# A mixture-of-experts kernel: guards moved behind another tile, eight index tiles, another order of an output's products

## The chip, the cores and the metric

The kernel runs on one core of a Trainium2 chip. The metric is the device time of one execution in microseconds (us). The kernel before took 802.78 us (median of three runs: 800.07, 802.78 and 802.8 us).

A core has five engines that run at the same time, each through its own list of instructions in order: PE (TensorE, matrix products), DVE (VectorE), ACT (ScalarE), POOL (GpSimd) and SP (SyncE, which here only issues DMAs). An instruction that must wait for another engine or for a DMA holds up everything behind it on its own engine.

## The reference, cut to what matters

The first half is a recurrence over 768 steps for 4 x 8 heads of 40 numbers; its output, laid out as 3072 rows of 320, goes into a mixture of eight experts:

```
state = state * w[t] - outer(state @ a[t], b[t]) + outer(v[t], k[t])
y[t]  = r[t] @ state                       # 4 x 8 heads, 40 x 40 state
x     = y as [3072, 320]
logits= x @ w_gate + log1p(exp(x @ w_noise)) * noise
top2  = the two best of 8 experts; weights = softmax over the two
for e in range(8): for k in range(2):
    rows = top2[:, k] == e
    out[rows] += weight[rows] * (relu(x[rows] @ w1[e]) @ w2[e])   # 320 -> 1024 -> 320
```

## The kernel before, in words

The recurrence fills the first 400 us of the span. The experts follow, from about 400 to 788 us, and a short check (`verdict`) ends the program. The change lies in the experts.

**Numbers in two halves.** Every float32 operand of the experts is split into two float16 tiles, a high part and a low part (the rest): the weights of the first product into `w1h` and `w1l`, of the second into `w2h` and `w2l`, the rows into `xh`, `xl` and, for the last 64 of the 320 columns, `x3` and `x3l`, the hidden layer into `hh` and `hl`. A product is then a sum of high by high, high by low and low by high.

**Tiles of an expert.** An expert has room for 832 rows in two parts (`PARTS`): 384 rows (part 0) and 448 rows (part 1). For each part `hidden` computes eight blocks of 128 hidden columns. A block (`block`, L348 to L357) is eight matmuls into one PSUM tile `ph` (three buffers): two of `wh` by `xh`, one by `x3`, two of `wl` by `xh`, two of `wh` by `xl`, one by `x3l`. ACT makes `hh` of it (L356), DVE makes `hl` (L357), and with that the buffer is free for the block that is three later. `trans` and `turn` transpose the rows on PE (L335, PSUM `pt`, two buffers), ACT makes `xh` and `x3` (L338, L341), DVE `xl` and `x3l` (L339, L342). `split1` and `split2` split weights (ACT L284 and L295, DVE L285, L286 and L296).

**Output tiles.** `output` goes over an expert's rows in tiles of 128, with one of 64 at the end. `otile` (L362 to L375) sums 24 matmuls of 128 by 320 in PSUM `po` (three buffers): eight of `hh` by `wh`, eight of `hl` by `wh`, eight of `hh` by `wl`. The 64-row tile does it in halves, 48 matmuls of 160 columns. ACT scales the sum by the row's weight into `y` (L372), and POOL adds `y` into the output in DRAM by a scatter with row indices (`add`, L378). For the 64-row tile, whose two halves lie on different partitions, DVE first computes an index tile `ix` (L374) out of the expert's row list: a tile called `ix2` of the pool `my`, which has two buffers. A third one can so be written only when the scatter of the first has landed.

**Row lists.** A list tile `le` holds an expert's row numbers and weights. It has three buffers and is filled by four small DMAs on SP (`lists`, L307: two for the 128-row tiles, two for the 64-row tile). POOL's `gather` (L313) fetches the rows by it.

**Guards.** Beside the sums run checks that the float16 halves are good enough: `sized` (L239, a maximum of a tile into `mx`), `finite` and `check1` (L242, a sum over the low parts into `yc`), and `flag` (L390 to L412: small operations on DVE named `ok`, `fz` and `g`, and small matmuls). Nothing waits for their results before the verdict.

**Order.** The names in the trace are those of memory: for even experts W1's halves and the rows read `rk` and `rw__68`, for odd ones `la`, `X__71` and `dr`; `ra` is W2 of expert 0. Of the experts the programmer writes only dependences and a few places; the order on each engine is chosen by the framework's scheduler when the program is built, which simulates the program by costs of its own. Places are given by `after(i, e)`, a dependence of one instruction upon another, and by `with issue_after(i):`, which lets the scheduler put what is inside only behind `i`. In `rest` (L438 to L464) the guards of the first expert stand in three such blocks, held behind `hx`:

```
s.trans(x[0],0,X,1); hx=s.hx3.ins; H1=s.hidden(W1,X,1,p)
with after(hx):
    for i in range(2): s.sized(s.x[i][0][:,0])
with after(hx): s.check1(W1)
      with after(hx): s.flag(s.pt,"pt",2,gam)
```

There `s.hx3` is the last DVE instruction that wrote `x3l`, that of expert 0, part 1.

Of the kernel before, what the change touches and what calls it, by code (L numbers as in the profile page):

```python
# [11 lines left out]
I32 = mybir.dt.int32  # L12
AF = mybir.ActivationFunctionType
ALU = mybir.AluOpType
# [38 lines left out]
class Moe:  # L53
# [275 lines left out]
    def after(s,i,e): s.tc.add_manual_dep(i.ins,e.ins.name,mybir.DependencyInfo(mybir.DependencyClass.Sync,mybir.DependencyReason.DATA),reason="place")  # L329
# [32 lines left out]
    def otile(s,W,H,wi,part,t,p,po,y):  # L362
        nc=s.nc; wh,wl=W; hh,hl=H; _,w_,idx=wi[:3]
        t0=s.parts[part][0]%CAP
        r=slice(t-t0,t-t0+p); ii=t//128
        c=128//p; d=DM//c
        k=0
        for h,w in ((hh,wh),(hl,wh),(hh,wl)):
            for f in range(8):
                for j in range(c): nc.tensor.matmul(po[p*j:p*j+p,:d],h[:,f,r],w[:,f,d*j:d*j+d],start=k==0,stop=k==23)  # L370
                k+=1
        s.hy=nc.scalar.activation(y[:,:d],po[:,:d],AF.Copy,scale=w_[:,ii:ii+1])  # L372
        if c==1: return s.out_d,idx[:,ii],y
        ix=s.yp.tile([128,1],I32,name="ix2"); nc.vector.scalar_tensor_tensor(ix,idx[:,ii],2.0,s.half2,op0=ALU.mult,op1=ALU.add)  # L374
        return s.out_d.rearrange("n (j d)->(n j) d",j=2),ix,y[:,:d]  # L375
    def add(s,o,e):
        s.finite(o[2])
# [60 lines left out]
    def rest(s,W1,W1n,W2,W2n,X,Xn,x,xn,ll,gam):  # L438
        after=s.tc.issue_after; p=s.places[5::2]; s.output(W2n,s.H,xn,1,0,p)
        for i in range(5): s.after(s.piece1(2,i),p[i])  # L440
        s.trans(x[0],0,X,1); hx=s.hx3.ins; H1=s.hidden(W1,X,1,p); s.after(s.piece1(2,5),p[5])
        for k,g in enumerate(s.gather(1,xn,1)): s.after(g,p[3+k])
        with after(s.hmm.ins): s.trans(xn[0],1,Xn,1)
        s.output(W2,H1,x,0,1)
# [3 lines that stand above are left out]
        W1,X,W2,x=W1n,Xn,W2n,xn  # L448
        for e in range(1,E_):
            if e+1<E_:  # L450
              r1=s.load1(e+1) if e>1 else s.w1s
              xn=s.loadx(e+1,places=p[7:10] if e==1 else ()); s.loadx(e+1,xn,1,p[10:] if e==1 else ()); r2=s.load2(e+1) if e>1 else s.r2
            if e>1: H0=s.hidden(W1,X,0)
            H1=s.hidden(W1,X,1); W1o=W1
            if e+1<E_: W1=s.split1(r1,e+1); X=s.trans(xn[0],e+1); s.trans(xn[0],e+1,X,1)
            if e>1: s.output(W2,H0,x,e,0)
            if e==1:
              with after(hx): s.flag(s.pt,"pt",2,gam)
            s.output(W2,H1,x,e,1); s.check1(W1o)
            if e+1<E_: W2=s.split2(r2,e+1); x=xn  # L460
# [651 lines left out]
```

## Time and profile before

| | |
|---|---|
| profiled execution | 800.72 us |
| its span, first to last instruction | 798.9 us |
| mean granted TensorE clock (share of full speed) | 0.974 |
| PE busy | 728.6 us, 91% of the span, 12622 matmuls |
| DVE busy | 495.0 us, 62% |
| ACT busy | 401.9 us, 50% |
| POOL busy | 348.7 us, 44% |
| blocks' matmuls L355 | 97.0 us + 86.4 us in two groups |
| PE po L370 on the chain that ended last | 21% of the span |

The span is 1.82 us shorter than the time of the execution. Busy shares are averages over two very different halves: in the first the engines hand small results to each other, in the second PE is the engine that others serve. The rows below say, for single instructions or for runs of equal ones (x24 is 24 of them), when the run began, how long it took, and in square brackets how long the engine stood idle before it and what ended that.

### The profile page before, as it was taken

What the parts mean: (1) busy time and instruction counts of PE and PEld (TensorE: products, weight loads), DVE (VectorE), ACT (ScalarE), POOL (GpSimd) and SP (SyncE); (2) the same over time, 40 slices, a digit from 0 to 9 for tenths busy, and PEclk for the clock granted to TensorE, in tenths of its full rate; (3) what the DMA queues carried; (4) which work ended last, traced back from release to release, by engine and by line L of the source; (5) the groups of instructions that cost most, each with busy time, mean ns of one, the idle gap of its engine ahead of it and who ended that gap; (6) DMA issues with size and microseconds to landing.
All of it is one profiled execution on the core that took longest, in us unless ns stands there. A gap on an engine that the chain in (4) does not pass through costs nothing.

```text
span 798.9 us, 29160 instructions
## 1 busy us (share of the span) xinstructions
PE 728.6 (91%) x12622; PEld 532.5 (67%) x12622; DVE 495.0 (62%) x1059; ACT 401.9 (50%) x876; POOL 348.7 (44%) x470
## 2 busy tenths in 40 slices
PE   7579999999999999898889898999999999999993
PEld 4367778888877777676655465657566675766662
DVE  7926667677989857935564675856565654652221
ACT  6765667676757444455442254454335434442220
POOL 9922143345367444325257544416345251503223
PEclk9699999999999999999999999999999999999997
DMA  6452344545544632352316664626445162402113
GB/s 203 149 133 70 100 143 149 157 143 162 156 132 127 196 104 58 105 154 66 93 58 128 140 145 125 152 77 130 125 112 142 41 143 71 50 5 34 22 21 39
DMA packets 67700, 87.07 MB, mean 109 GB/s; under 512 B 15640, under 2 KB 52460, under 8 KB 67564
## 3 DMA queue, kind: packets, MB, share of 16 engines
q1 hardware_dynamic: 55404, 67.98, 29.0%
q0 software_dynamic: 12160, 17.15, 12.8%
q8 instruction: 101, 1.65, 0.9%
q14 instruction: 35, 0.29, 0.1%
HBM read 63.41 MB, written 21.69 MB: 107 GB/s over the span
## 4 chain that ended last, share of the span: by engine, by line
PE 74%; ACT 9%; DVE 8%; issue 4%; DMA 2%; another core or an unknown queue 1%; POOL 1%; SPq 0%; ACTq 0%; DVEq 0%; POOLq 0%
PE po L370 21%; PE ph L355 20%; PE py L793 4%; PE pp L777 4%; PE rl L808 2%; PE pt L335 2%; PE sm L596 2%; PE tb L708 2%; ACT la L526 2%; PE ta L698 2%; PE kt L722 2%; ACT dr L526 2%; PE pw L739 2%; ACT tt L526 1%; PE pw L730 1%
## 5 line engine op out<-in xcount | busy, mean ns | idle before, releaser
L378 POOL DMA_INDIRECT out_dram<-y,le x45 | 74.5, 1656 | 176.4 <-ACT y L372 173.0
L355 PE MATMUL ph<-rw__68,rk 128*128 128x384 f16 (+1 forms) x512 | 97.0, 339 | 2.9 <-DVE hl L357 1.8
L355 PE MATMUL ph<-dr,la 128*128 128x448 f16 (+1 forms) x384 | 86.4, 341 | 1.7 <-DVE rk L357 1.2
L370 PEld LDWEIGHTS <-rk 128*128 128x128 f16 x576 | 56.1, 99 | 31.1 <-ACT rk L356 2.8
L355 PEld LDWEIGHTS <-rk 128*128 128x128 f16 x512 | 49.5, 98 | 39.4 <-issue 3.3
L182 POOL DMA_INDIRECT ls<-ent,po x48 | 49.6, 1034 | 54.3 <-ACT pm L526 33.3
L357 DVE SCALAR_TENSOR_TENSOR hl<-ph,hh 128x448 f16<-128x448 f32 x64 | 39.4, 621 | 49.9 <-ACT hh L356 49.2
L372 ACT ACTIVATE y<-po,le 128x320 f32<-128x320 f32 (+1 forms) x53 | 26.6, 504 | 86.7 <-PE po L370 77.3
L356 ACT ACTIVATE hh<-ph 128x448 f16<-128x448 f32 x64 | 34.2, 542 | 68.6 <-PE ph L355 64.8
L356 ACT ACTIVATE rk<-ph 128x384 f16<-128x384 f32 x64 | 30.9, 488 | 60.6 <-PE ph L355 48.5
L618 POOL TENSOR_TENSOR rk<-rk,B 104x512 f32<-104x512 f32 x34 | 40.4, 1191 | 42.8 <-DVE lg L812 41.3
L370 PEld LDWEIGHTS <-hh 128*128 128x128 f16 (+1 forms) x640 | 46.6, 103 | 18.7 <-issue 1.8
L646 DVE TENSOR_TENSOR Tt<-X__71 128x30 f32<-128x30 f32 (+9 forms) x150 | 54.3, 362 | 3.7
L355 PEld LDWEIGHTS <-la 128*128 128x128 f16 x384 | 37.5, 98 | 28.3 <-issue 2.6
L242 DVE TENSOR_REDUCE yc<-y 128x1 f32<-128x320 f32 (+1 forms) x53 | 23.8, 456 | 49.3 <-ACT y L372 49.2
L647 DVE TENSOR_TENSOR X__71<-X__71,Tt 128x30 f32<-128x30 f32 (+9 forms) x150 | 50.7, 338 | 5.5
L357 DVE SCALAR_TENSOR_TENSOR rk<-ph,rk 128x384 f16<-128x384 f32 x64 | 34.4, 552 | 31.2 <-ACT rk L356 25.1
L793 PE MATMUL py<-pm,kt 128*64 128x104 f32 (+1 forms) x768 | 43.5, 261 | 6.1 <-issue 4.6
L370 PE MATMUL po<-ra,rk 128*128 128x320 f16 x288 | 45.7, 305 | 2.9 <-ACT rk L356 2.4
L793 PEld LDWEIGHTS py<-pm,kt 128*64 128x64 f32 x768 | 36.7, 142 | 10.5 <-issue 7.4
L779 DVE TENSOR_TENSOR pm<-pp,mk 128x1024 f32<-128x1024 f32 x24 | 29.4, 1223 | 19.0 <-PE pp L777 18.2
L313 POOL DMA_INDIRECT rk<-xd,le x28 | 28.1, 1005 | 24.5 <-ACT hh L356 6.7
(330 smaller groups left out, 1726.1 us busy)
## 6 DMA issues: line engine op xcount, KB each, us to landing
rk<-in_gkb_dram SPq DMA_DIRECT2D x48, 160.0 KB
w2r<-in_w_dram SPq DMA_DIRECT2D x6, 1280.0 KB
w1s<-in_w_dram SPq DMA_DIRECT2D x28, 256.0 KB
xd<-xr SPq DMA_DIRECT2D x40, 160.0 KB
w1s<-in_w_dram SPq DMA_DIRECT2D x5, 1024.0 KB
out_dram<-z SPq DMA_DIRECT2D x15, 320.0 KB
rw__68<-in_gw_dram SPq DMA_DIRECT2D x24, 160.0 KB
ra<-in_ga_dram SPq DMA_DIRECT2D x48, 80.0 KB
```

Source lines behind the costliest of these rows:

```text
L182: st=nc.gpsimd.indirect_dma_start(out=s.ls,out_offset=OFFS(ap=po[:,j,k:k+1],axis=0),in_=s.ent[:,j,k],in_offset=None)
L355: for i,(a,b) in enumerate(mm): s.hmm=nc.tensor.matmul(ph[:,:n],a,b,start=i==0,stop=i==7)
L356: s.hrelu=nc.scalar.activation(hh[:,f],ph[:,:n],AF.Relu)
L357: s.hhl=nc.vector.scalar_tensor_tensor(hl[:,f],ph[:,:n],0.0,hh[:,f],op0=ALU.max,op1=ALU.subtract)
L370: for j in range(c): nc.tensor.matmul(po[p*j:p*j+p,:d],h[:,f,r],w[:,f,d*j:d*j+d],start=k==0,stop=k==23)
L378: st=s.nc.gpsimd.indirect_dma_start(out=o[0],out_offset=OFFS(ap=o[1],axis=0),in_=o[2],in_offset=None,compute_op=ALU.add)
L526: s.ea=s.nc.scalar.activation(*a,**k)
L618: s.after((eng or s.nc.gpsimd).tensor_tensor(z,z,b1,op=ALU.mult),e)
L646: eng.tensor_tensor(t,X[:,j:j+1,j+1:].to_broadcast([128,j,m]),X[:,0:j,j:j+1].to_broadcast([128,j,m]),op=ALU.mult)
L647: s.hs=eng.tensor_tensor(X[:,0:j,j+1:],X[:,0:j,j+1:],t,op=ALU.add)
L777: nc.tensor.matmul(pp[o:o+64,y,64*j:64*j+64],lh,r[Y,j],start=True,stop=True)
L793: nc.tensor.matmul(pp[64*y:64*y+64,b,128*hh:128*hh+n],kt[:,j,y],m[:,y,j,0:n],start=first and hh==0,stop=True,skip_group_check=True)
```

## The change

Three edits. In `otile` the products of an output tile come in the order high by high, `hh` by `wl`, `hl` by `wh`, where `hl` came second. The index tile `ix2` gets eight buffers of its own. And `hx` is taken behind `s.hidden(W1,X,1,p)`, as `s.hhl`, the DVE instruction that wrote the last `hl` of expert 0, part 1 (L357).

```
-        for h,w in ((hh,wh),(hl,wh),(hh,wl)):
+        for h,w in ((hh,wh),(hh,wl),(hl,wh)):
             for f in range(8):
                 for j in range(c): nc.tensor.matmul(...)
...
-        ix=s.yp.tile([128,1],I32,name="ix2"); nc.vector.scalar_tensor_tensor(ix,idx[:,ii],2.0,s.half2,...)
+        ix=s.yp.tile([128,1],I32,name="ix2",bufs=8); nc.vector.scalar_tensor_tensor(ix,idx[:,ii],2.0,s.half2,...)
...
-        s.trans(x[0],0,X,1); hx=s.hx3.ins; H1=s.hidden(W1,X,1,p); s.after(s.piece1(2,5),p[5])
+        s.trans(x[0],0,X,1); H1=s.hidden(W1,X,1,p); hx=s.hhl.ins; s.after(s.piece1(2,5),p[5])
```

The number of instructions stays the same; the scheduler puts them in another order on PE, DVE and ACT, and in the same order on POOL and SP.

On DVE, around the last blocks of expert 0, part 1 (`hl_8525`; the first two rows are transposed rows of that part), before:

```order
L339 SCALAR_TENSOR_TENSOR rw__68<-pt,rw__68 128x448 x2
L342 SCALAR_TENSOR_TENSOR rw__68<-pt,rw__68 64x448 x2
L239 TENSOR_REDUCE mx<-rk 128x1
L239 TENSOR_REDUCE mx<-rw__68 128x1
L242 TENSOR_REDUCE yc<-rk 128x1
L242 TENSOR_REDUCE yc<-rk 64x1
L390 MEMSET ok 128x5
L392 TENSOR_TENSOR fz<-acc 128x128
L402 TENSOR_TENSOR g_8959<-gam 128x216
L357 SCALAR_TENSOR_TENSOR hl_8525<-ph,hh_8524 128x448 x3
L393 TENSOR_SCALAR fz<-fz 128x128
```

The same place on DVE now (`dr` are rows of expert 1, part 1; `rk<-w1s` is the split of expert 2's W1):

```order
L357 SCALAR_TENSOR_TENSOR hl_8525<-ph,hh_8524 128x448 x8
L239 TENSOR_REDUCE mx<-rk 128x1
L239 TENSOR_REDUCE mx<-rw__68 128x1
L242 TENSOR_REDUCE yc<-rk 128x1
L242 TENSOR_REDUCE yc<-rk 64x1
L390 MEMSET ok 128x5
L392 TENSOR_TENSOR fz<-acc 128x128
L339 SCALAR_TENSOR_TENSOR dr<-pt,dr 128x448
L402 TENSOR_TENSOR g_8959<-gam 128x216
L339 SCALAR_TENSOR_TENSOR dr<-pt,dr 128x448
L285 SCALAR_TENSOR_TENSOR rk<-w1s,rk 128x1024 x2
```

All eight `hl` now come ahead of the guards, and the guards among the work for experts 1 and 2.

On DVE, where the weights of an odd expert have been split and the rows of the next are being transposed (`dr`), before (the index tile `ix_11058` is that of expert 5):

```order
L296 SCALAR_TENSOR_TENSOR w2l<-w2r,w2h 128x640 x4
L242 TENSOR_REDUCE yc<-y 128x1
L357 SCALAR_TENSOR_TENSOR rk<-ph,rk 128x384 x2
L374 SCALAR_TENSOR_TENSOR ix_11058<-le,half_606 128x1
L357 SCALAR_TENSOR_TENSOR rk<-ph,rk 128x384
L339 SCALAR_TENSOR_TENSOR dr<-pt,dr 128x384 x2
```

The same place now (`ix_11543` is the index tile of expert 6):

```order
L296 SCALAR_TENSOR_TENSOR w2l<-w2r,w2h 128x640 x2
L357 SCALAR_TENSOR_TENSOR rk<-ph,rk 128x384
L296 SCALAR_TENSOR_TENSOR w2l<-w2r,w2h 128x640 x2
L374 SCALAR_TENSOR_TENSOR ix_11543<-le,half_606 128x1
L357 SCALAR_TENSOR_TENSOR rk<-ph,rk 128x384 x2
L339 SCALAR_TENSOR_TENSOR dr<-pt,dr 128x384 x2
```

The index tile of the next expert stands where this expert's stood, and one `rk<-ph` (the low part `hl` of expert 4's block, L357) less stands ahead of it. The same shift by one expert is found at the other experts.

## Rows read from the trace of the kernel before

**Rows 1.** Waits of PE, 385 to 800 us: total us, times, longest.
```profile
PE po L370 <- ACT rk L356: 2.4, 1, 2.4
...
PE pt L335 <- DVE rw__68 L339: 2.2, 1, 2.2
PE ph L355 <- DVE hl L357: 1.8, 1, 1.8
...
PE ph L355 <- DVE rk L357: 1.2, 1, 1.2
```
**Rows 2.** A stretch: busy us by engine (count), granted clock, DMA share, GB/s.
```profile
600.00:650.00 50.00, 50.00 (x399) 32.88 (x398) 28.27 (x46) 22.90 (x42) 20.35 (x15) 1.00 0.46 105
```
**Rows 3.** Waits of DVE, 400 to 800 us, for the index tiles.
```profile
DVE ix L374 <- DMA out_dram<-y,ix: 9.8, 6, 2.3
```
**Rows 4.** Timeline of PE around the last blocks of expert 0.
```profile
455.52 4.70 PE L355 MATMUL ph<-rw__68,rk 128*128 128x448 f16 x24 [1.76 <-DVE hl L357]
...
463.89 1.37 PE L335 MATMUL pt<-idm,rw__68 128*128 128x128 f32 x8
...
479.86 0.73 PE L355 MATMUL ph<-dr,la 128*128 128x448 f16 x3
...
483.83 0.90 PE L335 MATMUL pt<-idm,rk 128*128 128x128 f32 x3 [2.21 <-DVE rw__68 L339]
...
487.12 0.73 PE L355 MATMUL ph<-dr,la 128*128 128x448 f16 x3
...
490.55 0.73 PE L355 MATMUL ph<-dr,la 128*128 128x448 f16 x3
```
**Rows 5.** Three short stretches, columns as in rows 2.
```profile
410.00:415.00 5.00, 3.85 (x22) 2.42 (x23) 3.23 (x9) 2.51 (x5) 0.00 (x0) 0.69 0.01 3
450.00:455.00 5.00, 3.50 (x20) 1.60 (x19) 4.86 (x8) 1.42 (x3) 2.49 (x4) 1.00 0.49 130
...
484.00:490.00 6.00, 6.00 (x28) 3.25 (x29) 4.06 (x8) 1.71 (x4) 4.68 (x5) 0.75 0.99 336
```
**Rows 6.** Timeline of DVE, 449 to 484 us.
```profile
449.76 0.49 DVE L239 TENSOR_REDUCE mx<-rk 128x1 f32<-128x320 f32 x1
...
454.84 1.69 DVE L357 SCALAR_TENSOR_TENSOR hl<-ph,hh 128x448 f16<-128x448 f32 x3
456.44 0.21 DVE L393 TENSOR_SCALAR fz<-fz 128x128 f32<-128x128 f32 x1
...
457.83 0.61 DVE L357 SCALAR_TENSOR_TENSOR hl<-ph,hh 128x448 f16<-128x448 f32 x1
...
464.81 2.36 DVE L285 SCALAR_TENSOR_TENSOR rk<-w1s,rk 128x1024 f16<-128x1024 f32 x2 [1.43 <-ACT rk L284]
...
476.13 1.27 DVE L342 SCALAR_TENSOR_TENSOR dr<-pt,dr 64x448 f16<-64x448 f32 x2 [0.48 <-issue]
...
480.38 0.32 DVE L242 TENSOR_REDUCE yc<-y 128x1 f32<-128x160 f32 x1
483.03 0.16 DVE L374 SCALAR_TENSOR_TENSOR ix<-le,half 128x1 int32<-128x1 int32 x1 [2.33 <-DMA out_dram<-y,ix]
483.22 0.56 DVE L339 SCALAR_TENSOR_TENSOR rw__68<-pt,rw__68 128x384 f16<-128x384 f32 x1
```
**Rows 7.** Timeline of ACT, the last `hh` of expert 0.
```profile
465.63 0.52 ACT L356 ACTIVATE hh<-ph 128x448 f16<-128x448 f32 x1
```
**Rows 8.** Timeline of DVE at a later index tile.
```profile
608.47 0.16 DVE L374 SCALAR_TENSOR_TENSOR ix<-le,half 128x1 int32<-128x1 int32 x1 [1.46 <-DMA out_dram<-y,ix]
```
**Rows 9.** Timeline of POOL before and behind that index tile.
```profile
601.34 1.55 POOL L378 DMA_INDIRECT out_dram<-y,le  x1 [1.83 <-ACT y L372]
...
608.04 1.01 POOL L313 DMA_INDIRECT rk<-xd,le  x1 [1.50 <-DMA le<-ls]
```
**Rows 10.** Timeline of SP there: list DMAs, then W2.
```profile
605.67 1.97 SPq L307 DMA_DIRECT2D le<-ls  x4
```
**Rows 11.** Timeline of PE there.
```profile
607.47 2.76 PE L355 MATMUL ph<-rw__68,rk 128*128 128x384 f16 x16
```

More of the change, by code (lines that the diff above doesn't have):

```diff
@@ L373, in otile @@
         if c==1: return s.out_d,idx[:,ii],y
-        ix=s.yp.tile([128,1],I32,name="ix2"); nc.vector.scalar_tensor_tensor(ix,idx[:,ii],2.0,s.half2,op0=ALU.mult,op1=ALU.add)
+        ix=s.yp.tile([128,1],I32,name="ix2",bufs=8); nc.vector.scalar_tensor_tensor(ix,idx[:,ii],2.0,s.half2,op0=ALU.mult,op1=ALU.add)
         return s.out_d.rearrange("n (j d)->(n j) d",j=2),ix,y[:,:d]
```

## The prediction

> **What bounds the kernel now.** I read the waits of PE first, for the stretch of the experts: only a handful is left, the four that matter here being 2.4, 2.2, 1.8 and 1.2 us [rows 1]. Then the busy time by stretches: from the second expert boundary on PE is busy 50.0 of 50 us while DVE works 28 [rows 2]. So in the second half PE sets the end, and a change is worth what it takes from, or adds to, PE's own waits. DVE's waits come next: index tiles held it up six times, 9.8 us in all, 2.3 at most [rows 3]. These are not PE's waits; they count only where PE is waiting for something queued behind them. Last I read the timelines around the two places where they do, and the granted clock of those places. The unit of all sums is the profiled execution, 800.72 us (span 798.9), which is 2.1 us below the median of the runs shown (802.78); the three runs lie 2.7 us apart.
>
> **Edit 1, the guards.** At 453.8 PE stands 1.76 us because a block's PSUM buffer waits for an `hl` [rows 4]. That `hl` came late because DVE worked on guards without a break from 449.76 to 454.84, 5.08 us [rows 6]. With all `hl` ahead of the guards this wait goes: the last block of expert 0 then ends at about 463.89 - 1.76 = 462.13 instead of 463.89 [rows 4].
>
> The guards don't go, they move. They are 5.08 us, and the six small pieces from 456.44 to 457.83, 1.39 us more [rows 6]; one piece of about 0.35 lands later, so 6.1 us now stand on DVE behind the last `hl`, in a stretch that was already dense. DVE had there, from 464.81 to the end of the row at 480.38 (480.70), 15.9 us with gaps of only 0.85 (0.48 shown, 0.37 of the like) and one `hl` of 0.62 that now comes earlier: 14.4 us of work [rows 6]. The last `hl` follows its `hh`, which ended about 466.1 [rows 7]; 1.76 earlier that is 464.3, and with 0.6 for `hl` DVE is free at 464.9. Then:
> - `x3l` of expert 1 (L342) ended at 477.40 [rows 6]. By the changed order 15.0 us of work lie up to its end, so 479.9. PE's first matmul that needs it is the second of the three that began at 479.86, near 480.05 [rows 4]; without the 1.76 PE comes there at 478.3. A wait of 1.6 us.
> - The `xl` for expert 2 (L339, 483.22 to 483.78) [rows 6] now ends at 464.9 + 14.4 + 6.1 + 0.56 = 485.9. PE's third group of transposes needs its buffer. PE came there at 483.83 - 2.21 = 481.62 [rows 4]; now at 481.62 - 1.76 + 1.6 + 0.8 (six output matmuls more stand ahead, at 0.136: sixteen of 384 columns took 2.6 [rows 11], 0.163 each, so 0.136 for 320 columns and 0.189 for 448) = 482.3. A wait of 3.6 us, where 2.21 were.
>
> In between, the index wait of 2.33 that delayed this L339 [rows 6] is gone in any case, see edit 2; DVE is late with work instead. From the end of expert 0's last block to the end of the row at 490.55 (491.12) PE had 27.2 us, of which 2.21 were the wait and about 1.6 a slow clock: the granted clock was 0.75 of full speed from 484 to 490 [rows 5], and PE took 3.3 us from 483.83 to 487.12 [rows 4] for matmuls worth 1.7 at their usual durations. So 23.4 us are work. The new end of that work is 462.13 + 23.4 + 1.6 + 3.6 = 490.7 at full clock, 0.4 earlier than before, and 492.3 with the same slow stretch, 1.2 later. The rows favour the second: after waits of 2.42 and 2.21 the clock fell (0.69 and 0.75), after one of 1.76 it did not (1.00) [rows 1, 5], and 3.6 is the longest of all. I take +1.2, with -0.4 and +2 (both waits half a microsecond longer) as ends.
>
> The Trainium skill, "TensorE: Matmul & The Clock Gate", section "HAM oscillation — how this bites in real kernels", says that waits between bursts of matmuls drop the clock to half and that each such wait pays the loss again. [...]
>
> **Edit 2, the index tiles.** With eight buffers an index tile no longer waits for the scatter two experts back. But each also moves one expert earlier in DVE's list, and what it reads is that expert's row list, which arrives just then: the wait gets another releaser. At the boundary near 602 the old wait ended at 608.47 [rows 8]. The new one ends when the list DMAs have landed. The four were issued from 605.67, 0.49 apart [rows 10], the first could be used by POOL's gather at 608.04 [rows 9], 2.4 later; the last, issued at 607.15, is there at 609.5: 1.05 us later than the old end. The order also puts seven matmuls of the next block, 7 x 0.163 = 1.14 us, ahead of the output tiles whose scatter (the one of 601.34) frees the list buffer [rows 9], so everything shifts to 610.7. Behind the index tile stands the `hl` of the second block (one `hl` less stands ahead of it now), done at about 611.4. PE needs that buffer for its fifth block, which began at 607.47 + 1.30 = 608.8 [rows 11]; three output matmuls more ahead make it 609.2. A new wait of 2.2 us where there was none.
>
> The other boundaries have the same shift with less behind it. Near 513 the index tile stands between two `hl`, 0 to 0.45 us. Near 558 the three matmuls put ahead delay lists and W2, and the existing wait of 1.2 at 569 [rows 1] grows by 0.25 to 0.6. Near 652 three `hl` are ahead of the index tile: nothing. The one near 700 disappears, but PE never waited there. Bounds of edit 2: from 0 (the list earlier than reckoned, or PE with other work) to 2.2 + 0.45 + 0.6 + 1.6 for a clock drop = 4.9. I take 2.2 + 0.3 = +2.5.
>
> The Trainium skill, "DMA: Bandwidth & Descriptors", section "Anatomy of one DMA", gives a small DMA about 2.0 us, nearly all of it until the write is confirmed. The 2.4 of the list here is close; by 2.0 the wait near 602 would be 1.8 instead of 2.2.
>
> **Edit 3, `hl` last in the sums.** Eight matmuls that need `hl` change places with eight that need `w2l`. No wait of PE on an output tile is put down to an `hl` within a sum: the one of 2.4 waits for `hh` [rows 1]. `w2l` is there earlier than needed. `w2h` is released eight matmuls later (1.1 us), and its next writer on ACT has slack in a stretch where ACT works under half the time [rows 2]. Zero, with -0.5 and +0.5 as ends.
>
> **Sum.** +1.2 + 2.5 + 0 = +3.7, so 800.72 + 3.7, about 804.5 us; on the level of the median it would be 806.5.
>
> **Rivals.**
> - A, faster: DVE keeps up, because guards slip into its gaps or parts run shorter, and the lists come in time. Then 1.76, 2.21 and the slow stretch of 1.6 all go: 800.72 - 5.6 = 795.2. For it: PE's head loses 5.6 us in just these. Against it: the dense stretch has 0.85 us of gaps for 6.1 of guards.
> - B, slower beyond the forecast: the clock falls at each wait that is made or grown, not only the longest. The place is the new wait near 602 and the grown one at 569, the price 1.6 each, the point from which it decides a wait between 1.76 and 2.21. 804.5 + 3.2 = 807.7. For it: 2.2 is as long as the wait that cost the clock before; against it: 1.2 + 0.3 is under 1.76.
> - C, nothing: the new waits eat what the old ones gave. Head -0.4 at full clock, the wait near 602 hidden since PE's fifth block also finds other work, +0.3 at 569: 800.6. For it: 50.0 of 50 us busy, so that little of what DVE does reaches PE.
>
> **How the numbers follow.** 0.5% is 4.0 us, about what a measurement of this kernel can tell from no change; against 802.78 the bounds are 798.8 and 806.8. Forecast (about 801.5 to 806.5 on the profile's level) 0.40, A 0.17, B 0.23, C 0.20. The forecast falls within the bounds for 0.28, and for 0.11 above if the runs lie on the median's level, 0.01 below; A is faster for 0.16 and within for 0.01; B slower for 0.20, within for 0.03; C within for 0.17, faster for 0.03. Together faster 0.20, same 0.49, slower 0.31. The range goes from 797, which leaves out most of A, to 810, B on the median's level; the forecast's own is 801.5 to 807.
>
> **What would show it.** Right: PE's 1.76 us wait gone and eight `hl` in a row ahead of the guards; a wait of PE of 3 to 4 us on L339 near 482 with a slow clock behind it, one near 478 on L342; DVE's index tiles waiting for `le` and no more for the scatter; a PE wait of about 2 us near 609 on an `hl`. Wrong: no wait of PE near 482, or one under 2 us, means DVE has slack that I did not see (A); an index tile that waits while PE has no wait near 609 is C; clocks under 1.00 near 569 and 611 are B. If the waits of PE sum to less than before and the time rises, the cause is none of these.

## The result and the profile after

The changed kernel takes 809.62 us (median of six runs, 809.06 to 815.41), the kernel before on the same chip 801.74 us (six runs): a ratio of 1.0115, 95% interval 1.0089 to 1.0141. It is slower, by more than forecast; 804.5 us was the forecast. On another chip the ratio was 1.0065 (1.0033 to 1.0096), see the fifth experiment. The profiled execution took 809.62 us with a span of 807.9 us, against 800.72 and 798.9 before. PE does the same 12622 matmuls and is busy for 730.8 us, 2.2 more than before; the larger part of the 9.0 us between the spans are its waits. Here are those in the part of the experts, 385 to 800 us (total us, times, longest):

```profile
PE ph L355 <- issue: 4.7, 3, 2.8
PE pt L335 <- DVE rw__68 L339: 3.6, 1, 3.6
PE ph L355 <- DVE rk L357: 2.7, 3, 1.7
PE po L370 <- ACT rk L356: 2.5, 1, 2.5
...
PE ph L355 <- DVE dr L342: 1.3, 1, 1.3
```

The 1.8 us on `hl` of [rows 1] is gone. In its place stand a wait on L342 and a longer one on L339; the wait of 1.2 us near 569 has grown to 2.8, and one of 1.7 near 617 is new. "issue" in the first row means that the trace names no releaser; what DVE did at the time of the longest one shows whose it is (below). The timeline of PE has the places in order:

```profile
481.25 0.73 PE L355 MATMUL ph<-dr,la 128*128 128x448 f16 x3 [1.34 <-DVE dr L342]
...
487.32 0.55 PE L335 MATMUL pt<-idm,rk 128*128 128x128 f32 x3 [3.57 <-DVE rw__68 L339]
488.38 0.77 PE L355 MATMUL ph<-dr,la 128*128 128x448 f16 x3 [0.52 <-DVE hl L357]
...
574.25 1.28 PE L355 MATMUL ph<-dr,la 128*128 128x448 f16 x3 [2.81 <-issue]
...
617.73 2.76 PE L355 MATMUL ph<-rw__68,rk 128*128 128x384 f16 x16 [1.73 <-DVE rk L357]
```

And DVE, which they wait for, at the same three places:

```profile
466.28 0.48 DVE L239 TENSOR_REDUCE mx<-rk 128x1 f32<-128x320 f32 x1
...
479.93 1.27 DVE L342 SCALAR_TENSOR_TENSOR dr<-pt,dr 64x448 f16<-64x448 f32 x2
...
486.70 0.56 DVE L339 SCALAR_TENSOR_TENSOR rw__68<-pt,rw__68 128x384 f16<-128x384 f32 x1
...
573.24 0.48 DVE L239 TENSOR_REDUCE mx<-w2r 128x1 f32<-128x320 f32 x1 [5.78 <-DMA w2r<-in_w_dram]
573.64 1.01 DVE L357 SCALAR_TENSOR_TENSOR rk<-ph,rk 128x384 f16<-128x384 f32 x2
...
617.04 0.16 DVE L374 SCALAR_TENSOR_TENSOR ix<-le,half 128x1 int32<-128x1 int32 x1 [1.92 <-DMA le<-ls]
617.12 1.01 DVE L357 SCALAR_TENSOR_TENSOR rk<-ph,rk 128x384 f16<-128x384 f32 x2
```

The guards start at 466.28, directly behind the last `hl`, and DVE works from there to 487.26 without a gap of even 0.2 us, where [rows 6] show it waiting before. At 573.24 a guard of another kind, the maximum over W2, stands in DVE's list in front of two `hl`; it had waited 5.78 us for the DMA, and the first `hl` behind it ends where PE goes on, at 574.2. At 617.04 the index tile of expert 6 ends a wait for the row list, no more for a scatter, with two `hl` behind it. The granted clock of three stretches behind these waits (columns as in [rows 2]):

```profile
487.00:493.00 6.00, 5.17 (x19) 2.45 (x20) 4.51 (x10) 1.51 (x3) 4.60 (x5) 0.72 0.93 299
574.00:580.00 6.00, 5.75 (x24) 2.76 (x24) 3.49 (x7) 1.38 (x3) 0.00 (x0) 0.72 0.01 3
617.50:623.00 5.50, 5.27 (x35) 3.41 (x35) 3.14 (x7) 2.50 (x5) 4.28 (x5) 1.00 1.02 354
```

The first has its counterpart in [rows 5] (0.75); the second is new and cost, by estimate, 0.28 x 6 = 1.7 us.

To compare kernels I use from here on the **experts' part**: from the PE row that follows a wait of 1.18 us on L341, which every one of the traces has (near 450 us, on the chip of the first four experiments near 429), to the start of the verdict's matmul (L422). The kernel before takes 789.10 - 448.48 = 340.6 us for it, the changed one 798.09 - 449.99 = 348.1. That is 7.5 of the 9.0 us between the spans. The other 1.5 lie ahead, and were 0.3 when the changed kernel was profiled again; and in the first four experiments the stretch from the first matmul of L155 to that row lasts 32.6 us each time, with one edit or with all three. So no effect of the change is seen there. Each experts' part comes from one profiled execution, and a slow clock that comes or stays away (last section) moves it by some 1.5 us; the times of the runs stand beside it.

### The profile page after: what moved, and what is told of

It is laid out like the page before. It is cut to its first block, busy times and chain, and to the rows that moved or that the text cites. A ratio compares the mean times of both kernels' runs of the same rounds, so it can differ in the third digit from the quotient of the medians.

```text
span 807.9 us, 29148 instructions
## 1 busy us (share of the span) xinstructions
PE 730.8 (90%) x12622; PEld 532.1 (66%) x12622; DVE 496.0 (61%) x1059; ACT 400.7 (50%) x876; POOL 345.5 (43%) x470
## 4 chain that ended last, share of the span: by engine, by line
PE 69%; ACT 10%; issue 8%; DVE 5%; POOL 4%; DMA 3%; another core or an unknown queue 0%; SPq 0%; ACTq 0%; POOLq 0%; DVEq 0%
PE ph L355 18%; PE po L370 18%; PE py L793 4%; PE pp L777 4%; PE rl L808 2%; PE sm L596 2%; PE tb L708 2%; ACT la L526 2%; ACT dr L526 2%; PE ta L698 2%; PE pt L335 2%; DMA out_dram<-y,le 2%; PE kt L722 2%; PE pw L739 2%; PE wm L574 2%
## 5 line engine op out<-in xcount | busy, mean ns | idle before, releaser
L355 PE MATMUL ph<-dr,la 128*128 128x448 f16 (+1 forms) x384 | 88.3, 346 | 7.6 <-issue 4.7
L370 PEld LDWEIGHTS <-rk 128*128 128x128 f16 x576 | 56.4, 99 | 31.3 <-ACT rk L356 2.9
L357 DVE SCALAR_TENSOR_TENSOR hl<-ph,hh 128x448 f16<-128x448 f32 x64 | 39.5, 623 | 56.7 <-ACT hh L356 54.7
L370 PEld LDWEIGHTS <-hh 128*128 128x128 f16 (+1 forms) x640 | 45.9, 103 | 18.8 <-issue 2.1
L357 DVE SCALAR_TENSOR_TENSOR rk<-ph,rk 128x384 f16<-128x384 f32 x64 | 34.3, 553 | 33.9 <-ACT rk L356 26.5
L370 PE MATMUL po<-ra,rk 128*128 128x320 f16 x288 | 46.1, 306 | 2.5 <-ACT rk L356 2.5
L793 PE MATMUL py<-pm,kt 128*64 128x104 f32 (+1 forms) x768 | 40.6, 254 | 5.4 <-issue 3.2
L793 PEld LDWEIGHTS py<-pm,kt 128*64 128x64 f32 x768 | 34.7, 137 | 8.7 <-issue 4.6
```

The lines of the kernel that those rows point to most:

```text
L355: for i,(a,b) in enumerate(mm): s.hmm=nc.tensor.matmul(ph[:,:n],a,b,start=i==0,stop=i==7)
L357: s.hhl=nc.vector.scalar_tensor_tensor(hl[:,f],ph[:,:n],0.0,hh[:,f],op0=ALU.max,op1=ALU.subtract)
L793: nc.tensor.matmul(pp[64*y:64*y+64,b,128*hh:128*hh+n],kt[:,j,y],m[:,y,j,0:n],start=first and hh==0,stop=True,skip_group_check=True)
```

## The experiments

Each was timed in five rounds beside the kernel before on the same chip; the experiments came on three chips, the first four on one where the kernel before takes 782.47 us instead of 801 or 802, so that ratios are compared, and the experts' part. The ratio is not the quotient of the two medians; where they differ, the ratio with its interval decides. The third and the fourth boundary between experts, named below, lie near 558 and 602 us in the kernel before. All numbers together:

| kernel | ratio to before (95% interval) | median us | before, us | experts' part, us |
|---|---|---|---|---|
| before | | | | 340.6 |
| changed | 1.0115 (1.0089 to 1.0141) | 809.62 | 801.74 | 348.1 |
| guards alone | 1.0022 (1.0000 to 1.0043) | 783.58 | 782.47 | 341.7 |
| index tiles alone | 0.9964 (0.9938 to 0.9989) | 779.46 | 782.47 | 337.0 |
| products alone | 1.0002 (0.9980 to 1.0024) | 782.38 | 782.47 | 341.3 |
| changed, W2 held | 1.0046 (1.0020 to 1.0073) | 784.78 | 782.47 | 343.2 |
| changed again | 1.0065 (1.0033 to 1.0096) | 807.10 | 800.57 | 349.0 |
| guards and index tiles | 1.0019 (0.9992 to 1.0046) | 802.34 | 800.57 | 344.1 |
| index tiles and products | 0.9974 (0.9949 to 0.9998) | 799.93 | 800.57 | 340.1 |
| index tiles, W2 held | 0.9927 (0.9903 to 0.9952) | 796.17 | 800.57 | 337.5 |
| changed, W2 and index held | 0.9986 (0.9961 to 1.0010) | 800.84 | 801.95 | 342.3 |
| changed, W2 held, flag late | 0.9986 (0.9965 to 1.0007) | 800.06 | 801.95 | 340.4 |
| index tiles, W2 held, guards early | 0.9912 (0.9876 to 0.9948) | 793.63 | 801.95 | 334.6 |

**1. The guards alone.**

```
-        s.trans(x[0],0,X,1); hx=s.hx3.ins; H1=s.hidden(W1,X,1,p); ...
+        s.trans(x[0],0,X,1); H1=s.hidden(W1,X,1,p); hx=s.hhl.ins; ...
```

> Only the guards moved, the index tiles and the order of the products as before. Theory D (DVE's dense stretch): the 1.76 us wait of PE on hl goes, a wait on L342 of about 1.3 and one on L339 of 3 to 4 us come, with a slow clock behind; 1 to 3 us slower than before, 802 to 804 where before is 801. Rival A (DVE has slack there): no wait on L339 over 2.2 us, 2 to 5 us faster, 796 to 799.

Measured: 1.1 us slower by the medians, the interval just reaching no change. PE's two waits:

```profile
462.20 0.73 PE L355 MATMUL ph<-dr,la 128*128 128x448 f16 x3 [1.88 <-DVE dr L342]
...
468.06 0.68 PE L335 MATMUL pt<-idm,rk 128*128 128x128 f32 x3 [3.36 <-DVE rw__68 L339]
```

The granted clock was 0.69 for the 5 us around the second. The waits are those of theory D; the gain from the 1.76 us wait is spent.

**2. The index tiles alone.** Only DVE's order differs from before.

```
-        ix=s.yp.tile([128,1],I32,name="ix2"); ...
+        ix=s.yp.tile([128,1],I32,name="ix2",bufs=8); ...
```

> Only the eight index tiles; PE, ACT, POOL and SP keep the order of before, only DVE's order differs. Theory L (the list takes the scatter's place and costs by what stands behind it): here three hl stand ahead of each index tile instead of one or two, so PE gets no new wait near 609; and without the index wait of 2.33 us ahead of L339 near 483 PE's wait of 2.21 and the slow clock behind it go: 2 to 4 us faster, 797 to 799. Rival M (an index tile on the list always costs): a PE wait of 1.5 to 2 us near 609 as in the changed kernel, and 1 to 3 us slower, 802 to 804.

Measured: 3.0 us faster by the medians, 0.36% by the ratio. DVE at the head of this kernel:

```profile
460.40 0.31 DVE L242 TENSOR_REDUCE yc<-y 128x1 f32<-128x160 f32 x1
460.74 0.56 DVE L339 SCALAR_TENSOR_TENSOR rw__68<-pt,rw__68 128x384 f16<-128x384 f32 x1
461.21 1.14 DVE L357 SCALAR_TENSOR_TENSOR hl<-ph,hh 128x448 f16<-128x448 f32 x2
463.63 0.16 DVE L374 SCALAR_TENSOR_TENSOR ix<-le,half 128x1 int32<-128x1 int32 x1 [1.27 <-DMA le<-ls]
```

L339 comes at once instead of behind an index tile, and PE's wait of 2.21 with the slow clock behind it is gone. The index tile still waits 1.27 us for its list, but behind the work that PE needs. Theory L holds: the list wait is not free or dear in itself, it costs by what stands behind it.

**3. The order of the products alone.**

```
-        for h,w in ((hh,wh),(hl,wh),(hh,wl)):
+        for h,w in ((hh,wh),(hh,wl),(hl,wh)):
```

> Only the order of the products in an output tile. Theory S (the scheduler's new places, seven matmuls of the next expert ahead of the outputs, delay what follows): near 570 PE waits 2 to 3 us instead of 1.2, with a slow clock behind it (1.6 us), and little else: 2 to 4 us slower, 803 to 805. Rival Z (the order of the products is free; all losses come from guards and index tiles): within 1 us of before. Rival H (the loss lies at 410 to 435 us, where the output tiles of the first expert changed): 2 to 3 us slower with longer waits of PE between 425 and 436, and the wait near 570 as before.

Measured: no difference. The waits moved: near 550 PE waits 2.17 us, as theory S had it, but without a slow clock; at the head L339's wait is 1.23 instead of 2.21, also without one; 0.56 is new at the fourth boundary; and 1.6 us were lost by a slow clock behind the 1.76 us on `hl`. Theory S is refuted in its size, Z is right in the time (the waits that came and went cancel), H is refuted (no wait between 390 and 420 us, where this chip has that stretch, is longer than in the first two experiments).

**4. The changed kernel with the maximum over W2 held.**

```
     def split2(s,w,e,hold=None):
...
-        s.sized(w[:,0])
+        with (s.tc.issue_after(hold) if hold else ExitStack()): s.sized(w[:,0])
...
-            H1=s.hidden(W1,X,1); W1o=W1
+            H1=s.hidden(W1,X,1); W1o=W1; hm_=s.hhl.ins
...
-            if e+1<E_: W2=s.split2(r2,e+1); x=xn
+            if e+1<E_: W2=s.split2(r2,e+1,hm_); x=xn
```

> The changed kernel, with the maximum over W2 (L239, mx of w2r) held back until the last hl of the expert's second part, so that DVE no longer stands in front of that DMA. Theory W (the wait of 2.8 us near 574 and the slow clock behind it come from DVE waiting 5.8 us for W2): both go, 4 to 5 us faster than the changed kernel, 804 to 806. Rival P (PE waits there for something else, since the trace names no releaser): that wait stays, within 1 us of 809.6.

Measured: 0.46% over before instead of 1.15 or 0.65; the interval overlaps with that of the second of these. On this chip the changed kernel itself was not run, so the gain is read from the experts' part: 343.2 against 348.1 and 349.0 us, 4.9 to 5.9 us. In the trace PE has no wait between 502 and 590 us; those of 1.34, 3.57 and 0.70 at the head, one of 0.60 near 501 and one of 1.52 at the fourth boundary are left. PE's order is that of the changed kernel but for five matmuls near 510 us. Theory W holds: the wait that had no releaser in the trace was DVE's wait for W2 (in experiments 6 and 7 the trace names it). The edit does one thing more: the tile `w2r` has one buffer, so the held maximum also holds back the next load, which is issued at 572.30 us here, 30 us behind the row lists instead of 2. DVE's place and the time of the load changed together.

**5. The changed kernel again.** No edit.

> The changed kernel once more, beside its pairs of edits and on one chip with them. Theory N (the three edits cost more together than alone: alone +0.2, -0.4 and 0%): its loss of about 1% over before is found again, 7 to 8 us, with waits of PE of about 3.6 on L339, 2.8 near the sixth block after the third expert boundary and 1.7 on hl at the fourth. Rival V (the loss of the first measurement was that chip's): 0 to 2.5 us over before, the sum of the edits alone or the time with W2 held.

Measured: 6.5 us over before by the medians, 5.2 by the ratio, a little less than theory N's 7 to 8 and above rival V's 2.5. The same waits, in the same places, that for W2 longer still:

```profile
573.69 1.28 PE L355 MATMUL ph<-dr,la 128*128 128x448 f16 x3 [3.71 <-DVE rk L357]
574.76 0.95 PE L355 MATMUL ph<-dr,X__71 128*128 128x448 f16 x2
...
577.42 1.32 PE L355 MATMUL ph<-dr,la 128*128 128x448 f16 x3
```

Three matmuls of 448 columns take 1.28 and 1.32 us here, and took 0.73 in [rows 4]: the clock was at the lower of its two levels, 0.50 granted over the 5.5 us that follow. DVE's W2 maximum ended its wait 10.15 us after SP issued the load (562.53 to 572.68); in the first profile of the changed kernel that was 9.26 us, in the kernel before 8.29, in the first three experiments 8.05 to 8.77, in the two pairs below 8.63 and 8.73.

**6. Guards and index tiles.** The edits of 1 and 2.

> Guards and index tiles, the order of the products as before. Theory N: the gain of the index tiles alone (3.0 us) came from L339 coming on time; with the guards in front of it, it is late whatever the index tile does, so the gain is lost: within 1.5 us of the guards alone, 0 to 2.5 us over before. Rival (the two add up): 2 us faster than before.

Measured: 1.8 us over before, the interval reaching from -0.6 to 3.7. The waits at the head are 1.88 and 3.37, with a clock of 0.72 behind them. The gain of experiment 2 (3.0 us) is lost as theory N says: with 6 us of guards in front of it L339 is late with or without the index tile's wait.

**7. Index tiles and products.** The edits of 2 and 3.

> Index tiles and order of the products, guards as before. Theory N: only with this order of DVE (one hl ahead of the index tile of expert 6 instead of three) does the list wait reach PE: a wait of 1.5 to 2 us on hl at the fourth boundary, and one of 2 to 3 us a boundary earlier, against the gain of up to 3.8 at the head; between 2 us faster and 2 us slower than before. Rival (the two add up): 3 us faster.

Measured: 2 us faster by the ratio, the upper end of its interval just under no change. The trace has the two waits that theory N asked for, 2.22 near 570 (1.24 before) and 1.53 at the fourth boundary, both with a granted clock of 1.00 behind them, and no wait on L339 at the head. Here the trace names the maximum over W2:

```profile
570.63 0.73 PE L355 MATMUL ph<-dr,la 128*128 128x448 f16 x3 [2.22 <-DVE mx L239]
```

The third pair, guards and products, was not run.

**8. Index tiles, W2 held.** The edits of 2 and 4, on the kernel before.

> The kernel before with the eight index tiles and with the maximum over W2 held behind the last hl of the second part, guards and products as before. Theory W: the wait of 1.55 us that is left with the index tiles alone near the third boundary goes too, and PE has no wait from the first boundary to the end: 4.5 to 5.5 us faster than before. Rival: W2's DMA is waited for elsewhere (its split), and the time is that of the index tiles alone, 3 us faster.

Measured: 0.73% faster, 4.4 us by the medians. The wait near 570 is gone, but PE waits 1.8 us in three pieces near 508 to 515: 0.98 and 0.51 on the flag's results, which lie in another place there, and 0.32 on a block's low part. (Nothing else uses these results before the verdict, but the flag's own small matmuls stand in PE's list and wait for them.) The experts' part is so that of experiment 2 (337.5 and 337.0); the intervals of the two ratios overlap, and whether the hold is worth anything by itself without the other edits stays open.

**9. The changed kernel, W2 held and each index tile held behind its own output tile's scaling.**

```
-... bufs=8); nc.vector.scalar_tensor_tensor(ix,...)
+... bufs=8); s.after(nc.vector.scalar_tensor_tensor(ix,...),s.hy)
```

> The changed kernel with the maximum over W2 held (as in the fourth experiment), and each index tile held behind the scaling (L372) of its own 64-row tile, so that DVE no longer stands in front of a list DMA. Theory L: the wait of 1.5 us on hl at the fourth boundary goes, all else stays: 1.5 to 2 us faster than with W2 held alone, 0 to 1.5 us over before. Rival: another wait takes its place at that boundary, and the time is that of W2 held alone, 2 to 3 us over before.

Measured: 1.1 us under before, interval from 3.1 under to 0.8 over. The wait of 1.52 at the fourth boundary is gone, and none took its place; the experts' part fell by 0.9 us. The ratio fell by 0.6% on another chip, which is more than that; why is not shown. The scheduler also changed PE's order, from about 545 to 710 us, so the hold alone is not all that differs.

**10. The changed kernel, W2 held, the flag in the fifth expert.**

```
-            if e==1:
-              with after(hx): s.flag(s.pt,"pt",2,gam)
+            if e==4:
+              with after(hm_): s.flag(s.pt,"pt",2,gam)
```

> The changed kernel with the maximum over W2 held, and the small operations of the flag (about 1.8 of the 6.1 us of guards) moved to the fifth expert; the maxima and sums over the low parts stay behind the last hl. Theory D (each us of guards in the dense stretch is a us of PE's wait there): the wait on L339 falls from 3.6 to about 1.8 us and that on L342 from 1.3 to about 0.7; 2 us faster than with W2 held alone, and 1.6 more if the slow clock goes too: 1.5 us under to 0.5 over before. Rival (the order alone sets these waits): the wait on L339 stays over 3 us.

Measured: 1.9 us under before by the medians; the interval holds no change. The two waits at the head:

```profile
480.16 0.73 PE L355 MATMUL ph<-dr,la 128*128 128x448 f16 x3 [0.22 <-DVE dr L342]
...
485.74 0.85 PE L335 MATMUL pt<-idm,rk 128*128 128x128 f32 x3 [3.08 <-DVE rw__68 L339]
```

I expected 0.7 and 1.8. The wait on L339 stayed over 3 us, which was the rival's mark, but the sum of the two fell from 4.91 to 3.30, 1.6 us for 1.8 us of guards taken away: as the first wait shrinks, PE comes to the second sooner. So each us of guards there cost PE about one; that it would be shared by the two waits in proportion was wrong. The experts' part fell by 2.8 us. Not all of that is the guards': PE's order differs from about 450 to 640 us, and the wait at the fourth boundary fell from 1.52 to 0.17 with the index tile where it was, its wait for the list 1.51 and two `hl` behind it. So that wait, too, hangs on PE's order as well as on DVE's.

**11. Index tiles, W2 held, guards early.** On the kernel of experiment 8: the maxima and sums over the low parts held behind the split of expert 1's W2 only, the flag in the fifth expert.

```
-            nc.vector.scalar_tensor_tensor(l[:,k:k+2],w[:,k:k+2],VE,h[:,k:k+2],...)      # split2
+            s.hw2=nc.vector.scalar_tensor_tensor(l[:,k:k+2],w[:,k:k+2],VE,h[:,k:k+2],...)
...
-        with after(hx): (both blocks, sized and check1)
+        with after(hw):      # hw=s.hw2.ins, taken at the start of rest
```

> The kernel before with eight index tiles and the maximum over W2 held (the eighth experiment), its guards moved the other way: the maxima and sums over the low parts held only behind the split of expert 1's W2, so that DVE does them near 436 to 444 us where it waits for outputs anyway, and the flag in the fifth expert. Theory D: the 1.76 us wait on hl goes and nothing comes in its place: 2 us faster than the eighth experiment, 6 to 8 us faster than before. Rival: the guards push the sums over y or the transposed rows near 445 us, PE waits there, and the time is that of the eighth experiment or above, 3 to 5 us under before.

Measured: ratio 0.9912 (0.9876 to 0.9948), 793.63 against 801.95 us. The lowest ratio of all, clear of both kernels; its interval overlaps with that of experiment 8. DVE does the guards here:

```profile
433.30 0.48 DVE L239 TENSOR_REDUCE mx<-rk 128x1 f32<-128x320 f32 x1
433.70 0.48 DVE L239 TENSOR_REDUCE mx<-rw__68 128x1 f32<-128x320 f32 x1
434.09 3.52 DVE L242 TENSOR_REDUCE yc<-rk 128x1 f32<-128x2048 f16 x2
...
443.28 1.31 DVE L339 SCALAR_TENSOR_TENSOR rw__68<-pt,rw__68 128x448 f16<-128x448 f32 x2
```

and behind the wait of 1.18 on L341 PE has none over 0.34 us up to the verdict. Its experts' part is 6.0 us shorter than that of the kernel before and 2.9 shorter than in experiment 8: the 1.76 us on `hl` and the 1.8 on the flag went, and 0.8 in three new small waits came. The guards themselves lie ahead of that part; from the output tiles (L370) near 432 us to its start PE takes 14.2 us, as in experiment 8, so they cost PE nothing there. PE's order differs from that of experiment 8 from about 450 to 640 us; what of the 2.9 us is due to that is not shown.

## Why the prediction was wrong

**What bounds the kernel, edit 1:** right. The two waits were forecast as 1.6 on L342 and 3.6 on L339; they are 1.34 and 3.57, the clock behind them is 0.72. The 1.76 us wait went. From the waits the head is 1.34 + 3.57 + 0.52 - 1.76 - 2.21 = 1.5 us worse and 0.2 more by the clock; the forecast was +1.2. Experiment 1 shows that the guards on DVE do it, and experiment 10 agrees that it is their amount. The weighing of the clock by the length of a wait fitted here, but it does not hold as a rule (last section). The row cited for the wait of 1.76 us, 450 to 455 us, ends before that wait does; the next one shows the same 1.00:

```profile
455.00:460.00 5.00, 4.48 (x24) 2.34 (x24) 4.04 (x11) 1.09 (x2) 2.34 (x3) 1.00 0.27 71
```

**Edit 2, the list in the scatter's place:** right in mechanism at the fourth boundary, 1.73 (1.55 in the second profile) where 2.2 was forecast. The price belongs to edits 2 and 3 together, though: alone, the index tiles stand behind three `hl` and cost nothing (experiment 2), and with the products' order PE and DVE are re-arranged so that one `hl` is ahead (experiment 7). I had put the seven early matmuls to edit 2; they come with edit 3. So the size came near with a part of the cause in the wrong place. The time of the list was right: the index tile's wait ended 2.2 us after the last of the four list DMAs was issued (614.82 and 617.04). The 2.0 us that I cited there from the Trainium skill, "DMA: Bandwidth & Descriptors", section "Anatomy of one DMA", stand for DMAs that GpSimd issues; the lists are issued by SP.

**The step that failed** is the term for the boundary near 558, "the existing wait of 1.2 at 569 grows by 0.25 to 0.6", taken as +0.3. It grew by 1.57 to 2.81 us, and the clock, whose fall there I had put at nothing, was 0.72 for the 6 us behind it, 1.7 more: 3.3 us instead of 0.3. The part that I had reckoned is there: SP issued the load of W2 3.86 us later than before (560.12 and 563.98) while PE came to the wait 3.27 us later (568.17 and 571.44), which is 0.6. The rest of it, 1.0, is the load, 9.26 us from issue to use instead of 8.29. I had taken its duration from before as fixed. Experiment 4 shows that the whole of it hangs on DVE standing in front of that DMA. Why the load takes longer is not shown. It is not the order at that place: from about 510 us on the changed kernel has the same order on PE, DVE, ACT and POOL as experiment 7, where the load took 8.73 us, PE waited 2.22 and the clock stayed at 1.00; and the two profiles of the changed kernel are themselves 0.9 us apart (9.26 and 10.15). In the trace of the changed kernel the 64-row scatter on POOL is issued at 561.55, 2.4 us ahead of the load, before at 556.93, 3.2 us ahead; that the two share DMA engines is argued from this, not tested.

**Edit 3, zero:** right alone in the time (ratio 1.0002), wrong in what it moves. Alone it already brings the wait for W2 to 2.17 us: the load takes 8.37 us there, as before, but PE comes to the wait 7.20 us after its issue instead of 8.05. Alone that is made up at the head, where L339's wait is 1.23 instead of 2.21; with the guards in the way it is not.

**The sum:** waits from 448 us on were 5.2 us before (1.76, 2.21, 1.24) and are 10.2 now (1.34, 3.57, 0.52, 2.81, 1.73, 0.27), +5.0; the slow clocks add 1.9; together 6.9 of the 7.5 us by which the experts' part grew. The last 0.6 I could not place. Rival B, the clock falling at a grown wait, was the nearest of the four cases with 807.7; its place near 569 was right, that near 602 was not (clock 1.00 behind 1.73 us). The single edits measured by themselves add up to -2.0 us by the medians: the loss is in their combination. One interaction is shown: with the guards in the way the index tiles' gain at the head is lost (experiments 2 and 6). A second is only seen: the wait for W2, 1.24 us before, 0.92, 1.55 and 2.17 with each edit alone, 1.57 and 2.22 in the two pairs, is 2.81 and 3.71 with all three, and only there does the clock fall. With one or two profiles of each kernel, and the same order there in experiment 7, it stays open whether the guards lengthen that load or whether it varies from one execution to the next.

## What to carry to other kernels

Work that nobody waits for still has a price: what stands behind it in its engine's list. Before such work is moved out of one engine's way, its total is to be laid beside the idle time of the place where it lands; here 6.1 us of guards went into 0.85 us of gaps, while near 433 us 4.3 us of them, with the flag in the fifth expert, cost PE nothing that shows. And an instruction that waits for a large DMA is best put behind everything that another engine needs, since the time of that DMA varied here from 8.05 to 10.15 us. In the changed kernel that was worth 4.9 to 5.9 us of the experts' part; in experiment 8, where the wait to be saved was 1.55, nothing beyond the noise.

## What the runs showed of the hardware that was not expected

**The clock does not follow from the length of one wait.** Behind the same wait of 1.76 us on `hl` the granted clock was 1.00 in the kernel before and in three experiments, and 0.69 in experiment 3, where 24 matmuls took 6.30 us instead of 4.70. The two kernels of experiments 3 and 7 even have the same order on PE throughout the experts. Waits of 2.17 and 2.22 us left it at 1.00, one of 2.21 brought 0.75. Between 411 and 415 us, where PE stands 2.4 us for an `hh` ahead of L370, the 17 matmuls behind it took 3.74 us in the kernel before and 2.48 in experiments 7 and 8. All waits of 2.8 us and more among the experts were followed by a stretch at 0.5 to 0.8. The row of PE in experiment 3, and the stretch, with the granted clock third from the end:

```profile
435.76 6.30 PE L355 MATMUL ph<-rw__68,rk 128*128 128x448 f16 x24 [1.76 <-DVE hl L357]
```

```profile
435.50:441.00 5.50, 5.24 (x20) 2.31 (x20) 3.25 (x10) 0.97 (x2) 1.64 (x2) 0.69 0.19 48
```

The Trainium skill, "TensorE: Matmul & The Clock Gate", section "HAM oscillation — how this bites in real kernels", describes a kernel that waits some 3 to 5 us between its bursts of matmuls and pays the lower clock again each time. The stretches behind the waits of 2.8 us and more agree with that; its kernel has no waits as short as those near 2 us, where both were measured here.

**Chips differ ahead of the experts.** On the chip of the first four experiments the kernel before took 782.47 us instead of 800.57 to 801.95, and the wait on L341 that marks the start of the experts' part ended near 429 us instead of 446 to 452. The experts' parts of the four kernels there, 337.0 to 343.2 us, lie among those of the other chips (334.6 to 349.0), so the difference lies ahead of that part. Why was not tested.
